# VectorE in source order from the first tile on, and weight halves without GpSimd: attention with a gated MLP on one core

## The chip, the cores and the metric

One core of a Trainium2 chip runs the whole program. The metric is device time in microseconds, the median of the runs of a kernel. All spans, busy times and waits below come from one profiled execution on that core.

## The reference

Attention with a bias that depends on the positions, then a gated MLP on its output. Cut to what matters:

```python
# q, k, v: (4, 8, 576, 64)   w_a, w_b: (512, 1536)   w_out: (1536, 512)
scores = scale * q @ k^T + bias            # bias: a small ReLU net of log1p|i-j| / log1p(i), per head
scores = scores - max(scores)
attn = exp(scores); attn = attn / (sum(attn) + 1e-9)
x = (attn @ v).transpose(0, 2, 1, 3).reshape(4 * 576, 512)
out = ((x @ w_a) * (x @ w_b)) @ w_out      # float32
```

## The kernel before, in words

**Number formats.** To get near float32 accuracy at a 16-bit matmul's pace, `x` and the weights of the MLP's first layer are kept as a scaled fp16 high part and an fp16 low part (the rest), and three products of such parts are added up (L767-771). The second layer does the same with 32-bit halves (`wos`, `gh`, `gl`). The scales are powers of two, found by `pow2_down` and `pow2_up` (L77-95): a maximum per partition, a small matmul that turns it, four tiny VectorE instructions, and a second small matmul with a table of ones (`one`, L877) that spreads the result.

**Attention.** The 144 tiles of 128 query rows run in the generator `attn_steps` (L661-736), two half steps per tile. Of tile n: `qk` makes the scores in PSUM (L502, L511, L525); `soft1` (L532) adds the bias, scales and takes the minimum in one VectorE instruction (L539) and the exponential with its sum on ScalarE (L544); `soft2` (L585) adds 1e-9 on GpSimd (L589), takes the reciprocal on VectorE (L590) and multiplies the tile on GpSimd (L595, for the first 48 tiles; later tiles are split into fp16 parts by L574 and L577); `turn` (L601) transposes the tile on TensorE (L607) and ScalarE copies it out; `pv` and `pv_first` multiply by v (L635, L556). The bias tiles come by DMA, a few tiles ahead.

**Weights.** The first layer's 24 chunks come as float64 and are turned into float32 on the chip. For each chunk `w_unit` (L263) lets ScalarE rescale the high words (L266) and VectorE shift and join bits (L268, L269, L272). `wab_size` (L284) takes the chunk's sum of absolute values on ScalarE (L289), and `wab_parts` (L302) makes the two fp16 parts: GpSimd scales the chunk in place (L306), ScalarE rounds it to fp16 (L309), GpSimd subtracts (L310). `wab_steps` (L320) runs these as a software pipeline of 31 steps. `wo_steps` then brings 12 chunks of the second layer, whose low part GpSimd makes too (L314).

**What sets the order.** Work of `attn_steps`, the weight steps and the MLP blocks (`moe_main`) is woven by `merge` in fixed proportions. TensorE issues in the order in which the program is written from the start (L856). For VectorE, ScalarE and GpSimd a scheduler orders the instructions when the program is built; VectorE too goes over to the written order towards the end of the second MLP block (L970), 46 tiles in. Two rules of `attn_steps` go with that: up to the tile `SOON = 46` the softmax's second half runs one tile late (L734-735), its transposes stand behind the next tile's `qk` (L711-713, L725-726), and the low parts of q, k and v are issued where they are made; from `SOON` on, `soft2(n)` stands ahead of `soft1(n + 1)` (L714-722), the transposes ahead of `qk` (L707-708), and the low parts are put off (`lows`). The first MLP block starts after tile 19, when 13 weight steps have been issued; the other 18 steps of the chunks are woven with its first 20 half steps and 27 half steps of attention (L936-938). Matmuls of `keep` (L885) fill TensorE up to there.

Of the kernel before, what the change touches and what calls it, by code (L numbers as in the profile page):

```python
# [28 lines left out]
FC = DFF // 128  # L29
# [21 lines left out]
SOON = 3 * N0 - 2  # L51
# [3 lines left out]
def attention_moe(ctx, tc, q0d, q1d, kd, vd, idn, wp, wa, wb, wo, lsw, lg, rl, out):  # L55
# [155 lines left out]
    def v_scale(b):  # L211
        mx = wtp[1].tile([128, NP], F32, tag="vmx", name="vmx", bufs=2)
        vfs = [load_v(b, hp) for hp in range(2)] if b else []
        yield
        for hp in range(NP):
            if b:
                junk = vf = vfs[hp]
            else:
                vf = st["vs", hp].rearrange("p x j d -> p (x j d)")
                junk = att.tile([128, 640], F32, tag="rv", name="junk", bufs=2)  # L220
            with late():
                nc.scalar.activation(junk, vf, AF.Abs, accum_out=mx[:, hp:hp + 1])
# [12 lines left out]
        vsc.append(v_scales(pow2_up(dg, 1, "v"), b))  # L235
        yield
# [26 lines left out]
    def w_unit(wt, raw, u=None):  # L263
        lo, hi = raw[:, :, 0], raw[:, :, 1]
        t = wt.tile([128, 512], I32, tag="wt", name="wt", bufs=4)
        nc.scalar.mul(t.bitcast(F32), hi.bitcast(F32), REBIAS)  # L266
        u, s = (t, hi) if u is None else (u, t)
        nc.vector.tensor_scalar(out=u, in0=t, scalar1=3, scalar2=None, op0=ALU.logical_shift_left)  # L268
        nc.vector.scalar_tensor_tensor(  # L269
            out=u, in0=lo, scalar=29, in1=u, op0=ALU.logical_shift_right, op1=ALU.bitwise_or  # L270
        )
        last.append(nc.vector.scalar_tensor_tensor(  # L272
            out=t, in0=s, scalar=-0x80000000, in1=u, op0=ALU.bitwise_and, op1=ALU.bitwise_or
        ))
        return t.bitcast(F32)
# [17 lines left out]
    def wab_scale(p, m):  # L293
# [4 lines left out]
            scalar1=vsc[0][1], scalar2=1.0 / PS, op0=ALU.mult, op1=ALU.mult,  # L298
# [3 lines left out]
    def wab_parts(p, c, wf, rm):  # L302
# [17 lines left out]
    def wab_steps(wt):  # L320
# [14 lines left out]
        fetch_to(3)  # L335
        yield
        for s in range(4 * np_ + 7):
            p, c = divmod(s - 7, 4)
            if 0 <= p < np_:
                if c == 0:  # L340
                    rms[p] = wab_scale(p, pow2_up(dgs.pop(p), 4, "w"))
                with late():
                    wab_parts(p, c, wfs.pop(s - 7), rms[p])
# [8 lines left out]
            if s < 4 * np_:  # L352
                wfs[s] = wab_conv(s, *raws.pop(s))
                fetch_to(s + 1 + min(6, 3 + s // 2))
            yield

    def wo_steps(wt):
        raws = [w_load(wt, wo, f) for f in range(2)]
        yield
        for f in range(FC):  # L360
            with late():
                wf = w_unit(wt, raws[f], wt.tile([128, 512], I32, tag="wt", name="wu", bufs=4))
                wo_split(f, wf)
# [42 lines left out]
    def prep_k(u):  # L406
# [44 lines left out]
    def prep_v(u):  # L451
# [209 lines left out]
    def attn_steps():  # L661
        vgen = [None]
        for n in range(NT + 4):
# [8 lines left out]
            if n <= SOON:  # L672
# [3 lines left out]
            for ahead, un in ((a, TILES[n + a][0]) for a in (6, 4, 3, 1, 0, -1) if 0 <= n + a < NT and FIRST[TILES[n + a][0]] == n + a):  # L676
# [7 lines left out]
                elif ahead == 3:  # L684
                    lows[0] = n >= SOON
# [21 lines left out]
            if SOON <= n < 3 * N0 + 2:  # L707
# [17 lines left out]
            if 2 <= n < SOON:  # L725
                turn(n - 2, tpp)
# [7 lines left out]
            if 1 <= n < SOON:  # L734
                run(soft2(n - 1))
# [135 lines left out]
    with tc.tile_pool(name="bg", bufs=1, side="right") as bg, tc.tile_pool(name="eq", bufs=1, space=PSUM) as eq, \  # L871
# [6 lines left out]
        nc.vector.memset(tab["one"], 1.0)  # L878
# [40 lines left out]
        with tc.tile_pool(name="bh", bufs=1, side="right") as bh:  # L919
# [5 lines left out]
            merge((units, NU0 // 2), (v_scale(0), 7), (wts, 2))  # L925
        keep(8)
# [36 lines left out]
    with tc.tile_pool(name="bg2", bufs=1, reuse_waits="tile") as bg:  # L963
# [6 lines left out]
        ctx.enter_context(tc.manual_schedule(engines={mybir.EngineType.DVE}))  # L970
# [66 lines left out]
```

## Time and profile before

| what | value |
|---|---|
| time, median of 3 runs (lowest, highest) | 752.47 us (751.37, 757.57) |
| the profiled execution's own time | 754.13 us |
| its span, first to last instruction | 752.3 us |
| TensorE matmul busy (share of the span) | 699.4 us (93%) |
| VectorE busy | 497.0 us (66%) |
| ScalarE busy | 449.1 us (60%) |
| GpSimd busy | 333.1 us (44%) |
| mean granted TensorE clock | 0.984 |

PE is TensorE's matmul stream and PEld its weight loads; DVE is VectorE, ACT ScalarE, POOL GpSimd. The granted clock is a share of full speed, 1.00 being 2.4 GHz and 0.50 being 1.2 GHz. A name such as L539 is a line of the kernel before. The shares are means over stages that differ, so the tables by stretch are the ones to read. A wait is put down to what came last: "PE qk L502 <- DVE mn L539" is TensorE standing still before its matmuls of line 502 until the VectorE instruction of line 539 is done.

### The profile page before, as it was taken

Reading aid. Unit: us, or ns where it says so; the run is one execution under the profiler, and the core shown is the slowest. Engines: PE = TensorE matmul, PEld = TensorE weight load, DVE = VectorE, ACT = ScalarE, POOL = GpSimd, SP = SyncE. Lnnn points to the kernel's source line nnn. Section 1 sums busy time; section 2 is a strip of 40 time slices with the busy share of each in tenths; the row PEclk is TensorE's granted clock in tenths of the full one; section 3 lists DMA queues with packets and bytes.
Section 4 is the critical chain, followed back from the end, with each engine's and each line's share of the span. In section 5 each row is a group of like instructions: output and inputs, shape, how many; then the busy total and the mean of one; then the engine's idle time right before and its main releaser. Section 6 shows DMA issues by size and latency. Waiting matters only on the chain.

```text
span 752.3 us, 15601 instructions
## 1 busy us (share of the span) xinstructions
PE 699.4 (93%) x5451; PEld 533.1 (71%) x5451; DVE 497.0 (66%) x1204; ACT 449.1 (60%) x1005; POOL 333.1 (44%) x477
## 2 busy tenths in 40 slices
PE   7787898899899999998899989999999999999997
PEld 2255465577787556676787768878888887888886
DVE  7768688858984576766798888888987781111100
ACT  6868887877876678754555556656655562321310
POOL 3437668865863123332354445634553562311200
PEclk9979999999999999999999999999999999999999
DMA  8998776477754887799999999999999974000001
GB/s 247 322 370 279 241 224 212 147 256 251 248 149 119 219 200 195 187 201 204 246 251 253 225 274 244 248 228 276 246 236 271 222 142 130 1 1 29 2 15 42
DMA packets 178163, 147.69 MB, mean 196 GB/s; under 512 B 125092, under 2 KB 138148, under 8 KB 178084
## 3 DMA queue, kind: packets, MB, share of 16 engines
q1 hardware_dynamic: 170928, 130.92, 69.4%
q10 hardware_dynamic: 5876, 10.93, 5.3%
q0 software_dynamic: 1280, 4.84, 1.8%
q8 instruction: 43, 0.70, 0.4%
q14 instruction: 36, 0.29, 0.1%
HBM read 101.15 MB, written 17.18 MB: 157 GB/s over the span
## 4 chain that ended last, share of the span: by engine, by line
PE 57%; DVE 11%; issue 9%; ACT 9%; POOL 7%; DMA 6%; SPq 0%; ACTq 0%; POOLq 0%; DVEq 0%
PE ab L768 25%; PE o L812 14%; PE pv L635 5%; PE qk L511 4%; DMA pt<-ph 3%; PE psta L155 3%; POOL ph L574 2%; DMA bias<-bias_d 2%; DVE p L539 2%; ACT p L544 2%; PE pr L888 2%; DVE wt L272 2%; PE tp L607 2%; DVE w16t L269 1%; POOL gl L788 1%
## 5 line engine op out<-in xcount | busy, mean ns | idle before, releaser
L768 PEld LDWEIGHTS <-w16t 128*128 128x128 f16 x2592 | 247.1, 98 | 47.1 <-issue 15.8
L768 PE MATMUL ab<-x,w16t 128*128 128x256 f16 x2304 | 270.4, 273 | 3.6 <-DVE x L650 3.3
L544 ACT ACTIVATE p<-p,mn 128x576 f32<-128x576 f32 x144 | 111.6, 775 | 72.9 <-DVE mn L539 63.1
L539 DVE CUSTOM_DVE_ANT_0 p<-qk,bias 128x576 f32<-128x576 f32 x144 | 107.3, 746 | 27.7 <-PE qk L511 11.5
L577 DVE SCALAR_TENSOR_TENSOR ph<-p,sm,ph 128x64 f16<-128x64 f32 x192 | 109.0, 608 | 20.6 <-POOL ph L574 20.0
L574 POOL TENSOR_SCALAR ph<-p,sm 128x576 f16<-128x576 f32 x96 | 71.5, 745 | 115.0 <-DVE sm L590 102.5
L812 PE MATMUL o<-wos,gh 128*128 128x512 f32 x384 | 120.3, 394 | 0.0
L788 POOL TENSOR_TENSOR gl<-g,gh 128x256 fp32r<-128x256 f32 x96 | 73.2, 762 | 89.9 <-ACT gh L787 89.9
L589 POOL TENSOR_SCALAR sm<-sm 128x1 f32<-128x1 f32 x144 | 59.0, 410 | 104.1 <-ACT p L544 99.8
L752 DVE SCALAR_TENSOR_TENSOR g<-ab,wv,asb 128x256 f32<-128x256 f32 x84 | 40.3, 480 | 81.9 <-ACT asb L776 80.7
L787 ACT CAST gh<-g 128x256 fp32r<-128x256 f32 x96 | 38.8, 404 | 75.8 <-DVE g L752 75.7
L812 PEld LDWEIGHTS o<-wos,gh 128*128 128x128 f32 x384 | 69.5, 188 | 16.0 <-issue 3.7
L511 PE MATMUL qk<-ks,qs 128*128 128x288 f32 x384 | 73.6, 313 | 6.0 <-DVE mn L539 4.2
L812 PE MATMUL o<-wos,gl 128*128 128x512 f32 x192 | 75.0, 391 | 0.0
L511 PEld LDWEIGHTS qk<-ks,qs 128*128 128x128 f32 x384 | 56.4, 190 | 16.1 <-DVE mn L539 5.8
L776 ACT ACTIVATE asb<-ab,wv 128x256 f32<-128x256 f32 x84 | 39.4, 469 | 29.0 <-PE ab L768 26.9
L595 POOL TENSOR_SCALAR p<-p,sm 128x576 f32<-128x576 f32 x48 | 43.9, 914 | 26.8 <-DVE sm L590 21.9
L635 PE MATMUL pv<-pt,vs 128*64 128x320 f16 (+1 forms) x560 | 43.5, 310 | 8.6 <-DMA pt<-ph 8.6
L635 PEld LDWEIGHTS <-vs 128*64 128x64 f16 x560 | 32.3, 115 | 21.3 <-issue 9.8
L607 PE MATMUL tp<-idn,p 128*128 128x128 f32 x240 | 38.3, 294 | 5.6 <-ACT ptf L612 4.1
L416 DVE TENSOR_TENSOR ks<-rk,ks 64x576 fp32r<-64x576 f32 x48 | 39.6, 824 | 3.7 <-ACT ks L419 2.2
L818 ACT COPY osb<-o 128x512 f32<-128x512 f32 x18 | 10.5, 583 | 52.2 <-PE o L812 36.4
(102 smaller groups left out, 964.2 us busy)
## 6 DMA issues: line engine op xcount, KB each, us to landing
bias<-bias_d SPq DMA_DIRECT2D x128, 288.0 KB, 3.9
rv<-vd SPq DMA_DIRECT2D x32, 320.0 KB, 4.5
rk<-kd SPq DMA_DIRECT2D x24, 288.0 KB, 3.3
wraw<-wa SPq DMA_DIRECT2D x12, 512.0 KB, 7.4
wraw<-wb SPq DMA_DIRECT2D x12, 512.0 KB, 5.7
wraw<-wo SPq DMA_DIRECT2D x12, 512.0 KB, 4.5
bias_d<-bo ACTq DMA_DIRECT2D x20, 295.5 KB, 3.7
bias_d<-bo POOLq DMA_DIRECT2D x16, 295.5 KB, 6.5
```

The costliest lines, as they stand in the source:

```text
L511: nc.tensor.matmul(ps[:, hf, :HB], a, b[:, hf * HB:hf * HB + HB], start=(x == 0), stop=(x == len(prods) - 1))
L539: ttr = nc.vector.tensor_tensor_reduce(out=p.rearrange("p (a n) -> p a n", a=2), in0=ps[:, :, :HB], in1=bt.rearrange("p (a n) -> p a n", a=2),
L544: exps.append(nc.scalar.activation(p, p, AF.Exp, bias=mn, scale=-1.0, accum_out=sm))
L574: nc.gpsimd.tensor_scalar(out=ph[:, :S], in0=p, scalar1=rc, scalar2=1.0, op0=ALU.mult, op1=ALU.mult)
L577: ins = nc.vector.scalar_tensor_tensor(out=ph[:, o:o + c1 - c0], in0=p[:, c0:c1], scalar=rc, in1=ph[:, c0:c1], op0=ALU.mult, op1=ALU.subtract,
L589: nc.gpsimd.tensor_scalar(out=sm, in0=sm, scalar1=1e-9, scalar2=1.0 / (PS if u >= NF else 1.0), op0=ALU.add, op1=ALU.mult)
L595: nc.gpsimd.tensor_scalar(out=p, in0=p, scalar1=rc, scalar2=1.0, op0=ALU.mult, op1=ALU.mult)
L607: nc.tensor.transpose(tp[:, x, :], p[:, c0:c0 + 128], tab["idn"])
L635: nc.tensor.matmul(ps[64 * j:64 * j + 64, o:o + N], v[:, j, :], p[:, j * N:j * N + N], start=(x == 0), stop=(x == len(prods) - 1),)
L768: nc.tensor.matmul(ab[:, j], w16[nm, f][:, pw, kk, :], xs[px][:, kk, :], start=(x % (3 * KC) == 0), stop=(x % (3 * KC) == 3 * KC - 1),)
L788: nc.gpsimd.tensor_tensor(out=gl, in0=g, in1=gh.bitcast(F32), op=ALU.subtract)
L812: nc.tensor.matmul(o, g[:, sl], wos[f][:, p], start=(f == 0 and x == 0), stop=(f == FC - 1 and x == 2))
```

## The change

Four things, in the words of the diff's names.

1. VectorE issues in written order from the first attention tile on, and the rules that held from tile 46 on hold from tile 0: `turn(n - 2)` ahead of `qk(n + 1)`, then `soft2(n)`'s start, `soft1(n + 1)`, the low parts put off.
2. The first ScalarE instruction of a weight chunk (`w_first`) is issued one step ahead of the chunk's VectorE instructions and writes straight into the tile that these then work on in place; the sign bits come from the raw chunk.
3. `wab_parts` uses no GpSimd: ScalarE multiplies by the scale while it rounds to fp16, and one step later VectorE makes the low part in one multiply-and-subtract. The factor 2^14 goes into the table of ones for that.
4. The weight pipeline gets one more step, and inside a step the chunk's conversion stands first.

```diff
@@ v_scales, tab["one"], wab_scale @@
-        nc.vector.tensor_scalar(out=inv, in0=m, scalar1=1.0 / PS, scalar2=None, op0=ALU.mult)
+        nc.vector.tensor_copy(inv, m)
...
-        nc.vector.memset(tab["one"], 1.0)
+        nc.vector.memset(tab["one"], 1.0 / PS)
...
@@ v_scale @@
         nc.vector.reduce_max(out=m1, in_=mx, axis=AX.X)
+        if b:
+            yield
         dg = pow2_down(m1, 1, "v")
         yield
-        if b:
-            yield
...
@@ weights @@
-    def w_unit(wt, raw, u=None):
-        lo, hi = raw[:, :, 0], raw[:, :, 1]
-        t = wt.tile([128, 512], I32, tag="wt", name="wt", bufs=4)
-        nc.scalar.mul(t.bitcast(F32), hi.bitcast(F32), REBIAS)
-        u, s = (t, hi) if u is None else (u, t)
-        nc.vector.tensor_scalar(out=u, in0=t, scalar1=3, scalar2=None, op0=ALU.logical_shift_left)
+    def w_first(raw, u):
+        nc.scalar.mul(u.bitcast(F32), raw[:, :, 1].bitcast(F32), REBIAS)
+        return u
+
+    def w_unit(raw, u, t):
+        lo, s = raw[:, :, 0], raw[:, :, 1]
+        nc.vector.tensor_scalar(out=u, in0=u, scalar1=3, scalar2=None, op0=ALU.logical_shift_left)
...
@@ wab_parts @@
-        nc.gpsimd.tensor_scalar(
-            out=wv, in0=wv, scalar1=rm[:, c:c + 1], scalar2=PS, op0=ALU.mult, op1=ALU.mult
+        nc.scalar.mul(hi, wv, rm[:, c:c + 1])
+        return lambda: nc.vector.scalar_tensor_tensor(
+            out=lo, in0=wv, scalar=rm[:, c:c + 1], in1=hi, op0=ALU.mult, op1=ALU.subtract
         )
-        nc.scalar.copy(hi, wv)
-        nc.gpsimd.tensor_tensor(out=lo, in0=wv, in1=hi, op=ALU.subtract)
...
@@ wab_steps @@
+        firsts = {0: wab_first(0, raws[0][1])}
         yield
-        for s in range(4 * np_ + 7):
+        low = None
+        for s in range(4 * np_ + 8):
             p, c = divmod(s - 7, 4)
+            if low:
+                low()
+                low = None
+            if s < 4 * np_:
+                pool, raw = raws.pop(s)
+                wfs[s] = wab_conv(pool, raw, firsts.pop(s))
+                pool = raw = None
+                fetch_to(s + 1 + min(6, 3 + s // 2))
+                if s + 1 < 4 * np_:
+                    firsts[s + 1] = wab_first(s + 1, raws[s + 1][1])
...
@@ attn_steps @@
-            if n <= SOON:
+            if n == 0:
                 soft1(n)
...
-            if SOON <= n < 3 * N0 + 2:
+            if 2 <= n < 3 * N0 + 2:
                 turn(n - 2, tpp)
...
-            if SOON <= n <= NT:
-                if n == SOON:
-                    run(soft2(n - 1))
+            if n <= NT:
                 s2 = soft2(n) if n < NT else iter(())
...
-            if 2 <= n < SOON:
-                turn(n - 2, tpp)
...
-            if 1 <= n < SOON:
-                run(soft2(n - 1))
...
@@ main program @@
             merge((units, NU0 // 2), (v_scale(0), 7), (wts, 2))
+        ctx.enter_context(tc.manual_schedule(engines={mybir.EngineType.DVE}))
         keep(8)
...
-        ctx.enter_context(tc.manual_schedule(engines={mybir.EngineType.DVE}))
         merge((main, 2 * FC - 22 + GS + 1), (asteps, n2 - n2 * 5 // 8))
```

VectorE where the first MLP block and the weight chunks run together, before (L268, L269 and L272 are the conversion of a chunk, L539 a tile's first softmax instruction, L590 its reciprocal):

```order
164 L268 TENSOR_SCALAR w16t<-wt 128x512
165 L539 ISA p,mn<-qk,bias 128x576
166 L539 ISA mn 128x1
167 L269 SCALAR_TENSOR_TENSOR w16t<-wraw,w16t 128x512
168 L268 TENSOR_SCALAR w16t<-wt 128x512
169 L272 SCALAR_TENSOR_TENSOR wt<-wt,w16t 128x512
170 L269 SCALAR_TENSOR_TENSOR w16t<-wraw,w16t 128x512
171 L590 RECIPROCAL sm<-sm 128x1
```

and the same place after (L311 is the new low part, L552 and L603 are the old L539 and L590, L80 to L86 the four small instructions of `pow2_down`):

```order
163 L311 SCALAR_TENSOR_TENSOR w16t<-wt,rm,w16t 128x512
164 L268 TENSOR_SCALAR w16t<-w16t 128x512
165 L269 SCALAR_TENSOR_TENSOR w16t<-wraw,w16t 128x512
166 L272 SCALAR_TENSOR_TENSOR wt<-wraw,w16t 128x512
167 L80 TENSOR_REDUCE p2m<-pr 4x1
168 L81 TENSOR_SCALAR p2m<-p2m 4x1
169 L82 TENSOR_SCALAR p2m<-p2m 4x1
170 L86 TENSOR_SCALAR p2d<-idn,p2m 4x4
171 L603 RECIPROCAL sm<-sm 128x1
172 L552 ISA p,mn<-qk,bias 128x576
173 L552 ISA mn 128x1
```

The instructions of two chunks and a tile are no longer mixed; a chunk stands in one piece with a low part in front, and a tile's reciprocal stands directly ahead of the next tile's first instruction.

TensorE near the end of the first stage, before (L502 makes the next tile's scores, L607 are the transposes of an earlier tile, L888 the filling matmuls):

```order
137 L888 LDWEIGHTS w16t
138 L888 MATMUL pr<-w16t 128x512
139 L502 MATMUL qk<-rkf,rqf 128x288 x2
140 L607 MATMUL tp<-idn,p 128x128 x5
141 L888 LDWEIGHTS w16t
```

and after (L620 is the old L607, L515 the old L502, L893 the old L888):

```order
139 L893 LDWEIGHTS w16t
140 L893 MATMUL pr<-w16t 128x512
141 L620 MATMUL tp<-idn,p 128x128 x5
142 L515 MATMUL qk<-rkf,rqf 128x288 x2
143 L893 LDWEIGHTS w16t
```

The transposes have moved ahead of the matmuls that wait for VectorE.

GpSimd in the stretch of the weight chunks, before (L306 and L310 make a chunk's parts, L589 and L595 belong to the softmax):

```order
59 L306 TENSOR_SCALAR wt<-wt,rm 128x512
60 L589 TENSOR_SCALAR sm<-sm 128x1
61 L595 TENSOR_SCALAR p<-p,sm 128x576
62 L310 TENSOR_TENSOR w16t<-wt,w16t 128x512 x2
63 L589 TENSOR_SCALAR sm<-sm 128x1
64 L595 TENSOR_SCALAR p<-p,sm 128x576
65 L306 TENSOR_SCALAR wt<-wt,rm 128x512 x3
```

and after (L602 and L608 are the old L589 and L595):

```order
47 L602 TENSOR_SCALAR sm<-sm 128x1
48 L608 TENSOR_SCALAR p<-p,sm 128x576
49 L602 TENSOR_SCALAR sm<-sm 128x1
50 L608 TENSOR_SCALAR p<-p,sm 128x576
51 L602 TENSOR_SCALAR sm<-sm 128x1
```

Only the softmax's two instructions per tile are left there.

## Rows read from the trace of the kernel before

**Rows 1.** Busy us by stretch: PE, PEld, DVE, ACT, POOL, clock, DMA share, GB/s.

```profile
36.00:62.00 26.00, 22.03 (x143) 13.93 (x139) 18.62 (x50) 18.12 (x43) 9.51 (x17) 0.80 0.92 338
62.00:99.30 37.30, 32.47 (x255) 19.49 (x255) 26.62 (x78) 32.37 (x76) 28.42 (x39) 1.00 0.81 264
99.30:138.60 39.30, 34.90 (x273) 24.02 (x270) 35.28 (x82) 31.10 (x71) 28.09 (x33) 1.00 0.66 208
138.60:166.50 27.90, 24.59 (x188) 18.45 (x188) 16.66 (x45) 22.98 (x49) 21.31 (x28) 0.94 0.61 203
166.50:235.00 68.50, 64.42 (x519) 52.69 (x520) 55.62 (x116) 52.12 (x111) 44.60 (x52) 0.98 0.69 214
235.00:330.00 95.00, 89.83 (x708) 59.95 (x706) 61.22 (x151) 69.71 (x151) 24.75 (x40) 1.00 0.78 184
```

**Rows 2.** TensorE's waits, 36 to 235 us: total us, times, longest us.

```profile
PE qk L502 <- DVE mn L539: 5.1, 3, 2.5
PE qk L511 <- DVE mn L539: 4.2, 4, 2.6
...
PE qk L525 <- DVE mn L539: 1.3, 2, 0.7
```

**Rows 3.** TensorE's waits, 235 to 330 us, the largest.

```profile
PE psta L155 <- DVE g L752: 1.7, 2, 1.2
```

**Rows 4.** VectorE by group, 99.3 to 138.6 us: busy us, mean ns.

```profile
L269 DVE SCALAR_TENSOR_TENSOR w16t<-wraw,w16t 128x512 int32<-128x512 int32 x11 | 9.9, 898 | 0.0
L272 DVE SCALAR_TENSOR_TENSOR wt<-wt,w16t 128x512 int32<-128x512 int32 x11 | 9.6, 872 | 0.0
L268 DVE TENSOR_SCALAR w16t<-wt 128x512 int32<-128x512 int32 x11 | 6.4, 579 | 1.8 <-ACT wt L266 1.8
...
L590 DVE RECIPROCAL sm<-sm 128x1 f32<-128x1 f32 x8 | 1.2, 153 | 1.7 <-POOL sm L589 1.7
```

**Rows 5.** Instructions in order of time, 129 to 134 us: start us, us.

```profile
129.37 2.79 POOL L310 TENSOR_TENSOR w16t<-wt,w16t 128x512 f16<-128x512 f32 x2
...
131.06 1.65 DVE L269 SCALAR_TENSOR_TENSOR w16t<-wraw,w16t 128x512 int32<-128x512 int32 x1
...
133.30 0.42 DVE L268 TENSOR_SCALAR w16t<-wt 128x512 int32<-128x512 int32 x1
...
133.64 0.68 DVE L272 SCALAR_TENSOR_TENSOR wt<-wt,w16t 128x512 int32<-128x512 int32 x1
```

**Rows 6.** GpSimd by group, 99.3 to 138.6 us.

```profile
L310 POOL TENSOR_TENSOR w16t<-wt,w16t 128x512 f16<-128x512 f32 x9 | 11.7, 1314 | 0.3
L595 POOL TENSOR_SCALAR p<-p,sm 128x576 f32<-128x576 f32 x8 | 7.9, 991 | 5.1 <-DVE sm L590 3.7 <-PE tp L607 1.4
L306 POOL TENSOR_SCALAR wt<-wt,rm 128x512 f32<-128x512 f32 x8 | 5.9, 744 | 3.9 <-DVE rm L295 3.9
L589 POOL TENSOR_SCALAR sm<-sm 128x1 f32<-128x1 f32 x8 | 3.1, 382 | 1.2 <-ACT p L544 0.6
```

**Rows 7.** VectorE by group and shape, whole run: the nearest form to the new instruction.

```profile
L577 DVE SCALAR_TENSOR_TENSOR ph<-p,sm,ph 128x512 f16<-128x512 f32 x96 | 71.4, 743 | 0.0
```

**Rows 8.** The first tile's softmax in order of time, 36 to 39 us.

```profile
36.47 0.76 DVE L539 CUSTOM_DVE_ANT_0 p<-qk,bias 128x576 f32<-128x576 f32 x1 [3.15 <-PE qk L525]
...
37.27 0.78 ACT L544 ACTIVATE p<-p,mn 128x576 f32<-128x576 f32 x1 [2.81 <-DVE mn L539]
...
38.24 0.19 POOL L589 TENSOR_SCALAR sm<-sm 128x1 f32<-128x1 f32 x1 [2.94 <-ACT p L544]
38.46 0.16 DVE L590 RECIPROCAL sm<-sm 128x1 f32<-128x1 f32 x1 [0.54 <-POOL sm L589]
```

**Rows 9.** VectorE's waits, 166.5 to 235 us, the largest.

```profile
DVE sm L590 <- POOL sm L589: 6.5, 6, 2.1
```

**Rows 10.** GpSimd by group, 166.5 to 235 us, the largest.

```profile
L314 POOL TENSOR_TENSOR wos<-wt,wos 128x512 fp32r<-128x512 f32 x12 | 18.2, 1523 | 5.0 <-ACT wos L313 5.0
```

More of the change, by code (lines that the diff above doesn't have):

```diff
@@ L50 @@
 VS = N0 - 4, 2 * N0 - 4, 3 * N0 - 10
-SOON = 3 * N0 - 2
 @with_exitstack
@@ L278, in attention_moe, with wab_first, wab_conv @@
     w16t = cst.tile([128, FC, 2, 2, KC, 128], F16, name="w16t")
-    def wab_conv(n, wt, raw):
+    def wab_first(n, raw):
         with late():
-            return w_unit(wt, raw, w16t[:, n // 2, n % 2].rearrange("p x k n -> p (x k n)").bitcast(I32))
+            return w_first(raw, w16t[:, n // 2, n % 2].rearrange("p x k n -> p (x k n)").bitcast(I32))
+    def wab_conv(wt, raw, u):
+        with late():
+            return w_unit(raw, u, wt.tile([128, 512], I32, tag="wt", name="wt", bufs=4))
     def wab_size(f, j, wf, m):
@@ L297, in wab_scale @@
             out=winv[:, 2 * p:2 * p + 2, :], in0=m.rearrange("p (f j) -> p f j", j=2),
-            scalar1=vsc[0][1], scalar2=1.0 / PS, op0=ALU.mult, op1=ALU.mult,
+            scalar1=vsc[0][1], scalar2=None, op0=ALU.mult,
         )
@@ L342, in wab_steps @@
                 with late():
-                    wab_parts(p, c, wfs.pop(s - 7), rms[p])
+                    low = wab_parts(p, c, wfs.pop(s - 7), rms[p])
             p, c = divmod(s - 5, 4)
@@ L351, in wab_steps, with first @@
                 wab_size(2 * p + c // 2, c % 2, wfs[s - 1], ms[p])
-            if s < 4 * np_:
-                wfs[s] = wab_conv(s, *raws.pop(s))
-                fetch_to(s + 1 + min(6, 3 + s // 2))
             yield
     def wo_steps(wt):
+        def first(f):
+            with late():
+                return w_first(raws[f], wt.tile([128, 512], I32, tag="wt", name="wu", bufs=4))
         raws = [w_load(wt, wo, f) for f in range(2)]
+        t = first(0)
         yield
@@ L361, in wo_steps @@
             with late():
-                wf = w_unit(wt, raws[f], wt.tile([128, 512], I32, tag="wt", name="wu", bufs=4))
+                wf = w_unit(raws[f], t, t)
                 wo_split(f, wf)
-            raws[f] = None
+            raws[f] = t = wf = None
             if f + 2 < FC:
                 raws.append(w_load(wt, wo, f + 2))
+            if f + 1 < FC:
+                t = first(f + 1)
             yield
     st = {}
-    lows = [False, []]
+    lows = []
     def lows_now(k=9):
-        for _ in range(min(k, len(lows[1]))):
-            lows[1].pop(0)()
+        for _ in range(min(k, len(lows))):
+            lows.pop(0)()
     def load_unit(u):
@@ L419, in prep_k @@
             nc.scalar.copy(ks[sl, j], rk[sl])
-            lows[1].append(partial(low, j))
-        if not lows[0]:
-            lows_now()
+            lows.append(partial(low, j))
         st["ks", u] = ks
@@ L433, in prep_q @@
         nc.scalar.copy(d[:, 0], s)
-        lows[1].append(
+        lows.append(
             lambda: nc.vector.tensor_tensor(out=d[:, 1], in0=s, in1=d[:, 0].bitcast(F32), op=ALU.subtract)
         )
-        if not lows[0]:
-            lows_now()
         st["qs", u] = dst
@@ L460, in prep_v @@
         nc.scalar.mul(hi, rv, vsc[UNITS[u][0]][0])
-        lows[1].append(lambda: nc.vector.scalar_tensor_tensor(
+        lows.append(lambda: nc.vector.scalar_tensor_tensor(
             out=lo, in0=rv, scalar=vsc[UNITS[u][0]][0], in1=hi, op0=ALU.mult, op1=ALU.subtract
         ))
-        if not lows[0]:
-            lows_now()
         st["vs", u] = vs
```

2 lines of the change are left out of this document (removed).

## The prediction, made before the changed kernel was run

> **What bounds the kernel now.** I read the table of busy time by stretch first, then each engine's waits in the stretches that the change touches, then the groups of VectorE and GpSimd there, and last the instructions in order of time around a few long ones. The stretches are cut close to where tiles 10, 20, 28, 34 and 48 begin.
>
> The table [rows 1] shows two kinds of stretch. From 235 us on, TensorE is busy 89.8 of 95 us, and the waits left there are small [rows 3]: nothing ahead of it is late. Between 36 and 235 us it is busy 178.4 of 199 us, so it stands still for 20.6, and at 0.80, 0.94 and 0.98 of the clock in three stretches it also runs below full speed. That is all that a better order can win, because the number of matmuls is the same after the change.
>
> Who makes it wait differs. From 99.3 to 138.6 us VectorE is busy 35.3 of 39.3 us [rows 1]: eight tiles, and eleven weight chunks to convert [rows 4]. VectorE is the bound of this stretch. From 138.6 to 166.5 us VectorE has little to do (16.7 of 27.9), while GpSimd is busy 21.3 and ScalarE 23.0. From 166.5 to 235 us TensorE is at 64.4 of 68.5 again. The waits agree: matmuls that wait for a tile's first softmax instruction cost TensorE 5.1, 4.2 and 1.3 us [rows 2], 10.6 in all.
>
> VectorE's own time is stretched by GpSimd. One L269 takes 1.65 us where it meets the subtraction L310, a like instruction 0.68 us where it does not [rows 5]. In the busy stretch the means of L269, L272 and L268 are 0.898, 0.872 and 0.579 us [rows 4]. Against 0.68, 0.68 and 0.42 [rows 5] this is 0.22, 0.19 and 0.16, times eleven 6.3 us.
>
> **The change part by part.** *GpSimd's share of the chunk parts goes to ScalarE and VectorE.* Removed are 24 each of L306 and L310. ScalarE's rounding stays and gets a factor, at no cost that I can see: it is one instruction on the same tile as before. Added are 24 multiply-and-subtract instructions on VectorE. The nearest form, with the same shapes and types, takes 0.743 us [rows 7], so 17.8 us in all. Counted in the order against the tiles, 5 of them fall in 62 to 99.3 us, 11 in 99.3 to 138.6 and 8 in 138.6 to 166.5.
>
> In the bound stretch this is 11 x 0.743 = 8.2 us. What comes back is the stretching by L306 and L310. They are 17.6 of GpSimd's 28.6 us there [rows 6], so I give them 62% of 6.3, or 3.9 us. VectorE's load becomes 35.3 + 8.2 - 3.9 = 39.6 us in a stretch of 39.3. So the stretch cannot get shorter, unless all the stretching goes (35.3 + 8.2 - 6.3 = 37.2, a gain of 2.1). It gets longer by as much of its present 4.0 us of VectorE's idle time as stays (43.6, a loss of 4.3). Some of these waits have lost their reason: the 1.8 us for ScalarE's first instruction, which is now a step ahead, and the 1.7 us for GpSimd [rows 4], which now has the softmax only. So I take +0.5.
>
> The lock between the two engines is also the place where the Trainium skill speaks against the change. Its page "SBUF — State Buffer", section "Who interferes with whom", says that a VectorE instruction with two inputs in SBUF and a GpSimd instruction that reads SBUF shut each other out for a whole instruction, and the new instruction is of that kind. The row of 1.65 us agrees with it [rows 5]. By the rule, if each of the 24 met a softmax multiplication L595 (0.991 us, [rows 6]) half way, 24 x 0.5 = 12 us would be added to the 17.8; the sum goes by the mean stretching in the rows instead.
>
> From 62 to 99.3 us, 5 x 0.743 = 3.7 us of new work stand against 10.7 us in which VectorE is idle [rows 1]. I take that as hidden and give the order -0.5 there (bounds -4.8, TensorE's idle time, and +3.7, all of the new work in the open). From 138.6 to 166.5 us, 8 x 0.743 = 5.9 us stand against 11.2 us of idle VectorE, and the queue of GpSimd, on which a tile's normalization had to wait behind L306 and L310, is gone. TensorE stands still for 3.3 us there, and 0.94 of the clock over 27.9 us is another 1.7. I take half of the two, -2.5 (bounds -5.0 and, with the new work uncovered, +5.9).
>
> *VectorE in written order; transposes ahead of the scores; the softmax's end ahead of the next tile.* The same rules hold before the change from tile 46 on, and there TensorE's waits for L539 are gone [rows 3]. The transposes now fill the time in which TensorE waited for L539. The price is that VectorE stands before the reciprocal of a tile until ScalarE's exponential and GpSimd's L589 are through, and all that follows is queued behind: the next tile's first instruction, hence TensorE's next scores. On the first tile this chain takes from 36.47 to 38.62 us, 2.15 us [rows 8], and a tile takes 2.6 us there (ten tiles start in the 26 us of that stretch). With a chunk's conversion between (0.42 + 0.68 + 0.68 = 1.8 us) most of the wait is covered. So the first stretch neither gains nor loses much by it: -0.5, with -4.0 (TensorE's idle time) and -5.2 (its clock) together as the lower bound and +2 as the upper, an estimate from ten tiles that each lose 0.2.
>
> From 166.5 to 235 us the chunks of the second layer are converted, GpSimd still makes their low parts, and only the order changes. TensorE's idle time is 4.1 us and its clock costs 0.02 x 68.5 = 1.4. I take -1.5 (bounds -5.5, and +8.7, worked out below).
>
> *Chunks one step ahead, one more weight step, the scale in the table of ones.* No instruction is added on the path. The parts of a chunk are ready four steps before the MLP asks for them, so one step later costs nothing; without that cover it would be one step, some 3 us, once. After 235 us nothing changes: 0 (bounds -1 and +1, since the loads on SP's queue keep nearly their order).
>
> Sum: -0.5 - 0.5 + 0.5 - 2.5 - 1.5 = -4.5 us. The profiled execution took 754.13 us (span 752.3 and 1.8 around it), so 749.6 for it. It lies 1.7 above the median of 752.47, and for a median I forecast **748.0 us**.
>
> **The rivals.** *A: the order works everywhere (738.8).* TensorE's waits for L539 go (10.6 us, [rows 2]) and with them the lower clock after 138.6 us (1.7 + 1.4): -13.7. For it: from 235 us on, the same order shows no such wait. Against it: there VectorE is busy 61 of 95 us, and in the bound stretch it is full.
>
> *B: VectorE becomes the bound for good (760.7).* Place: 99.3 to 138.6 us. The port that L306 and L310 leave is taken up by new meetings of the low parts with L595, nothing comes back, and 8.2 us stand in the open. It decides if the mean of L269 and L272 there stays near 0.88 us. For it: VectorE has 4 us left there, and a low part and a conversion in one piece, 2.5 us, stand ahead of each softmax. Against it: 62% of GpSimd's work there is gone.
>
> *C: VectorE stuck behind GpSimd's subtractions (some 758).* Place: 166.5 to 235 us. L314 takes 1.523 us, twelve times [rows 10]; six reciprocals wait behind GpSimd there for 6.5 us already [rows 9], 1.1 each. In the written order what follows cannot pass. If all 14 tiles wait so, 8 x 1.1 = 8.7 us more; with the 3 us that the other stretches give, +5.7. It decides if that wait doubles.
>
> *D: no change worth the name (752.5).* Chunks keep their places between the tiles almost to the tile in both orders, so the written order moves little, and VectorE's new load in the bound stretch eats what the next one gives.
>
> The Trainium skill would make the move itself dearer or cheaper by little: "GPSIMD Engine Reference", section "Performance versus the Vector engine", calls VectorE about twice as fast for such work, which from L310's 1.314 us [rows 6] would make the low part 0.66 and the 11 of them 7.2 us, not 8.2. No row here shows this instruction on VectorE yet.
>
> **How the numbers follow.** Forecast 0.40, A 0.18, B 0.11, C 0.09, D 0.22. A measurement of this kernel can tell about 1%, or 7.5 us, from no change. Faster by more: A, and a third of the forecast's spread, 0.31. Slower by more: B, and most of C, 0.20. The rest, 0.49, is within. The range from 739 to 760 leaves out the far half of A and of B.
>
> **What would show it.** Right: the mean of L269 and L272 in the chunk stretch falls to about 0.75 us, the new instruction takes about 0.74, VectorE is over 95% busy there; TensorE's waits for L539 shrink below 5 us; the stretch from tile 28 to tile 34 is 2 to 3 us shorter. Wrong: tiles 20 to 28 take more than 42 us (B), the wait for L589 after tile 34 grows beyond 10 us (C), or the time from tile 48 to the end is not what it was.

## The result, and the profile after

| | before | after |
|---|---|---|
| time, median of 4 runs (lowest, highest) | 754.73 us (751.37, 757.57) | 763.28 us (761.84, 765.37) |
| profiled execution, its span | 754.13, 752.3 us | 761.84, 760.0 us |
| VectorE, GpSimd busy | 497.0, 333.1 us | 507.6, 279.0 us |

The ratio is 1.0119, with a 95% interval from 1.0083 to 1.0155. The change makes the kernel slower by about 9 us, and 763 lies outside the range of 739 to 760.

In the code after, L515 and L552 are what L502 and L539 were before; likewise L576/L577 for L563/L564, L602/L603 for L589/L590, L608 for L595, L78 to L93 for L79 to L94, and L893 for the fillers L888. L310 is ScalarE's high part of a chunk and L311 the new low part on VectorE.

The busy time by stretch of the kernel after, cut where the tiles 10, 20, 28, 34 and 48 begin in it (columns as in [rows 1]):

```profile
64.60:110.80 46.20, 35.73 (x230) 20.45 (x227) 27.35 (x80) 30.16 (x68) 10.91 (x20) 0.82 0.60 195
110.80:154.70 43.90, 37.79 (x279) 26.24 (x278) 36.97 (x93) 33.65 (x75) 8.67 (x16) 0.92 0.59 188
154.70:176.80 22.10, 20.56 (x172) 16.09 (x171) 15.42 (x42) 19.30 (x42) 6.48 (x13) 1.00 0.58 176
176.80:248.20 71.40, 65.58 (x541) 52.95 (x539) 62.33 (x125) 54.09 (x115) 43.34 (x53) 1.00 0.70 227
```

Before, tile 10 began at 65.5 us and the same four pieces took 33.8, 39.3, 27.9 and 69.4 us. So tiles 10 to 20 lost 12.4 us, tiles 20 to 28 lost 4.6, tiles 28 to 34 won 5.8, and tiles 34 to 48 lost 2.0. What lies ahead won 0.9 and what lies behind 4.6; together +7.7, the difference of the spans. The forecast, in the same order, was -0.5 ahead of tile 10, then -0.5, +0.5, -2.5, -1.5 and 0. In the first two pieces no engine is full: VectorE is busy 27 of 46 and 37 of 44 us. The time went into waits and into a lower clock, 0.82 and 0.92.

TensorE's and VectorE's waits from 84 to 124 us, kernel after:

```profile
PE pr L893 <- DVE p2m L80: 4.4, 1, 4.4
PE pr L893 <- DVE p2g L93: 2.4, 1, 2.4
...
DVE p L552 <- PE qk L515: 7.4, 3, 3.0
DVE x L577 <- ACT x L576: 5.2, 2, 3.0
DVE w16t L311 <- ACT w16t L310: 1.9, 1, 1.9
```

Most of VectorE's 7.4 us for the scores lie behind TensorE's two standstills, not ahead of them. The kernel before has these two as well, but short (TensorE's waits from 65.5 to 99.3 us):

```profile
PE pr L888 <- DVE p2g L94: 0.8, 1, 0.8
...
PE pr L888 <- DVE p2m L81: 0.4, 1, 0.4
```

They have nothing to do with the softmax. They belong to the exchange of a scale between the partitions (TensorE transposes maxima by L78, VectorE reduces them by L80 to L86, TensorE spreads the result by L91, VectorE copies it by L93). It has one PSUM tile, `pr`, which the fillers use too. The largest wait in order of time, all engines, kernel after:

```profile
97.19 0.65 ACT L263 ACTIVATE w16t<-wraw 128x512 f32<-128x512 f32 x1
...
97.66 0.38 PE L78 MATMUL pr<-idn,vm 128*1 128x128 f32 x2
97.75 0.71 ACT L310 ACTIVATE w16t<-wt,rm 128x512 f16<-128x512 f32 x1
...
98.36 0.61 ACT L293 ACTIVATE w16t<-wt 128x512 f16<-128x512 f32 x1
...
98.97 0.35 ACT L576 ACTIVATE x<-pv,vs 128x128 f16<-128x128 f32 x1
99.35 0.35 DVE L577 SCALAR_TENSOR_TENSOR x<-pv,vs,x 128x128 f16<-128x128 f32 x1 [3.02 <-ACT x L576]
99.62 0.74 DVE L311 SCALAR_TENSOR_TENSOR w16t<-wt,rm,w16t 128x512 f16<-128x512 f32 x1
...
101.46 0.69 DVE L272 SCALAR_TENSOR_TENSOR wt<-wraw,w16t 128x512 int32<-128x512 int32 x1
102.07 0.27 DVE L80 TENSOR_REDUCE p2m<-pr 1x1 f32<-1x128 f32 x1
...
102.39 1.01 PE L893 MATMUL pr<-w16t 128*128 128x512 f16 x2 [4.36 <-DVE p2m L80]
...
103.20 1.27 PE L620 MATMUL tp<-idn,p 128*128 128x128 f32 x5
```

L78 is through at 98.04 us. Its answer L80 takes 0.27 us, and comes at 102.07. Ahead of it in VectorE's written order stands the low part of x, L577, which waits 3.02 us because ScalarE does three instructions for the chunks before L576; behind that come the low part of a chunk and a conversion, 2.7 us with L577. VectorE stands idle while L80 is ready. TensorE, whose order is written too, stands before the filler that needs `pr`, and the transposes and scores behind the filler wait with it. That VectorE takes its instructions strictly first in, first out is what the Trainium skill says too ("TensorE: Matmul & The Clock Gate", the table that opens it); the 4.0 us in which L80 was ready and did not run agree.

The first wait, 2.44 us, is for L93:

```profile
84.41 0.38 PE L91 MATMUL pr<-p2d,one 4*128 4x4 f32 x2
...
84.57 0.74 DVE L311 SCALAR_TENSOR_TENSOR w16t<-wt,rm,w16t 128x512 f16<-128x512 f32 x1
...
87.02 0.15 DVE L93 COPY p2g<-pr 128x4 f32<-128x4 f32 x1
...
87.23 1.01 PE L893 MATMUL pr<-w16t 128*128 128x512 f16 x2 [2.44 <-DVE p2g L93]
```

L91 is through at 84.79, and L93 comes at 87.02, behind a low part and a conversion; no input is late there, the work ahead is only long. After this wait four groups of matmuls run at half the clock: L893, L620, L515 and L569 take 1.01, 1.27, 1.33 and 2.60 us, where a kernel without this wait (below) has 0.59, 0.71, 0.76 and 1.46. That is 2.7 us more, so this wait costs about twice its length. After the second wait, of 4.36 us, the next four groups take 4.6 us instead of 2.7, 2.0 more. The granted clock is 0.50 from 87 to 93 us, and 0.73 from 84 to 104.

### The profile page after: what moved, and what is told of

Same layout as the page of the kernel before. It is cut to its first block, busy times and chain, and to the rows that moved or that the text cites. A ratio compares the mean times of both kernels' runs of the same rounds, so it can differ in the third digit from the quotient of the medians.

```text
span 760.0 us, 15593 instructions
## 1 busy us (share of the span) xinstructions
PE 699.6 (92%) x5451; PEld 532.2 (70%) x5451; DVE 507.6 (67%) x1228; ACT 450.9 (59%) x1005; POOL 279.0 (37%) x429
## 4 chain that ended last, share of the span: by engine, by line
PE 54%; DVE 11%; issue 11%; ACT 11%; POOL 7%; DMA 5%; SPq 0%; ACTq 0%; POOLq 0%; DVEq 0%
PE ab L773 23%; PE o L817 14%; PE pv L648 5%; POOL ph L587 4%; PE qk L524 3%; PE psta L154 3%; ACT p L557 2%; POOL sm L602 2%; DVE p L552 2%; POOL gl L793 1%; PE tp L620 1%; DVE ph L590 1%; ACT w16t L293 1%; ACT w16t L263 1%; DVE ks L435 1%
## 5 line engine op out<-in xcount | busy, mean ns | idle before, releaser
L552 DVE CUSTOM_DVE_ANT_0 p<-qk,bias 128x576 f32<-128x576 f32 x144 | 107.1, 744 | 26.5 <-PE qk L524 11.3
L590 DVE SCALAR_TENSOR_TENSOR ph<-p,sm,ph 128x64 f16<-128x64 f32 x192 | 109.3, 609 | 21.8 <-POOL ph L587 20.8
L602 POOL TENSOR_SCALAR sm<-sm 128x1 f32<-128x1 f32 x144 | 59.6, 414 | 126.9 <-ACT p L557 125.5
L524 PEld LDWEIGHTS qk<-ks,qs 128*128 128x128 f32 x384 | 56.2, 189 | 12.4 <-issue 5.4
L608 POOL TENSOR_SCALAR p<-p,sm 128x576 f32<-128x576 f32 x48 | 36.5, 761 | 73.9 <-DVE sm L603 72.4
L648 PE MATMUL pv<-pt,vs 128*64 128x320 f16 (+1 forms) x560 | 41.5, 301 | 6.8 <-DMA pt<-ph 6.8
L620 PE MATMUL tp<-idn,p 128*128 128x128 f32 x240 | 37.1, 288 | 10.4 <-ACT ptf L625 5.0
L620 PEld LDWEIGHTS tp<-idn,p 128*128 128x128 f32 x240 | 28.7, 148 | 18.6 <-issue 11.8
L817 PEld LDWEIGHTS o<-wos,gl 128*128 128x128 f32 x192 | 36.0, 188 | 7.8
```

The source lines that it names most:

```text
L524: nc.tensor.matmul(ps[:, hf, :HB], a, b[:, hf * HB:hf * HB + HB], start=(x == 0), stop=(x == len(prods) - 1))
L552: ttr = nc.vector.tensor_tensor_reduce(out=p.rearrange("p (a n) -> p a n", a=2), in0=ps[:, :, :HB], in1=bt.rearrange("p (a n) -> p a n", a=2),
L590: ins = nc.vector.scalar_tensor_tensor(out=ph[:, o:o + c1 - c0], in0=p[:, c0:c1], scalar=rc, in1=ph[:, c0:c1], op0=ALU.mult, op1=ALU.subtract,
L602: nc.gpsimd.tensor_scalar(out=sm, in0=sm, scalar1=1e-9, scalar2=1.0 / (PS if u >= NF else 1.0), op0=ALU.add, op1=ALU.mult)
L620: nc.tensor.transpose(tp[:, x, :], p[:, c0:c0 + 128], tab["idn"])
L648: nc.tensor.matmul(ps[64 * j:64 * j + 64, o:o + N], v[:, j, :], p[:, j * N:j * N + N], start=(x == 0), stop=(x == len(prods) - 1),)
```

## The experiments

The table has the kernel after (763.28 us, beside 754.73 before) and fourteen experiments, with ratios to runs of the kernel before on the same chip (median 754.5 for the first four experiments, 754.1 for the next four, 753.7 for four more, 755.3 for the last two). The kernel after, e1, e5 and e9 have four runs each, so their intervals are the widest; the others have eight or ten. The last columns say how much later than in the kernel before a tile begins, in the trace.

| kernel | median us | ratio (95%) | tile 20 | tile 34 | tile 143 |
|---|---|---|---|---|---|
| after | 763.28 | 1.0119 (1.0083 to 1.0155) | +11.5 | +10.3 | +7.8 |
| e1_order_only | 766.38 | 1.0173 (1.0107 to 1.0239) | +10.6 | +12.0 | +12.0 |
| e2_parts_only | 749.56 | 0.9945 (0.9921 to 0.9968) | +1.5 | -3.4 | -5.5 |
| e3_no_fill | 758.76 | 1.0064 (1.0036 to 1.0092) | +5.6 | +4.3 | +5.4 |
| e4_pow2_first | 762.02 | 1.0107 (1.0074 to 1.0140) | +9.6 | +8.7 | +9.0 |
| e5_x_late | 765.74 | 1.0166 (1.0112 to 1.0221) | +7.0 | +9.6 | +11.8 |
| e6_both | 757.67 | 1.0062 (1.0034 to 1.0089) | +3.6 | +2.5 | +3.3 |
| e9_rules_only | 745.24 | 0.9895 (0.9848 to 0.9942) | -1.8 | -6.7 | -8.8 |
| e8_from_19 | 754.81 | 1.0015 (0.9986 to 1.0043) | -1.1 | +0.2 | 0.0 |
| e10_low_mid | 751.35 | 0.9959 (0.9931 to 0.9986) | -1.5 | -5.5 | -3.3 |
| e11_until_19 | 757.64 | 1.0046 (1.0010 to 1.0083) | +8.4 | +3.5 | +4.9 |
| e12_all_mends | 758.76 | 1.0064 (1.0032 to 1.0097) | +3.1 | -0.2 | +4.7 |
| e13_no_order | 751.82 | 0.9969 (0.9943 to 0.9996) | -1.0 | -4.2 | +3.7 |
| e14_until_19_mended | 752.65 | 0.9967 (0.9936 to 0.9997) | +2.1 | +0.6 | -1.2 |
| e15_rules_mended | 747.99 | 0.9907 (0.9873 to 0.9942) | 0.0 | -2.8 | -3.1 |

**The two parts of the change, one at a time.** The kernel after with GpSimd making the chunk parts again:

```diff
-        nc.scalar.mul(hi, wv, rm[:, c:c + 1])
-        return lambda: nc.vector.scalar_tensor_tensor(
-            out=lo, in0=wv, scalar=rm[:, c:c + 1], in1=hi, op0=ALU.mult, op1=ALU.subtract
-        )
+        nc.gpsimd.tensor_scalar(
+            out=wv, in0=wv, scalar1=rm[:, c:c + 1], scalar2=1.0, op0=ALU.mult, op1=ALU.mult
+        )
+        nc.scalar.copy(hi, wv)
+        nc.gpsimd.tensor_tensor(out=lo, in0=wv, in1=hi, op=ALU.subtract)
```

> The changed kernel with the chunk parts made on GpSimd again (scale, round on ScalarE, subtract). Theory 1 (the written order makes VectorE read the small maxima in the one PSUM bank `pr` late, TensorE stands before the filling matmuls that use the same bank, and its clock falls): the loss stays, 760 to 766 us, and tiles 16 to 22 again take some 40 us instead of 25. Theory 2 (the 24 new low parts overload VectorE, rival B): the loss goes, 752 to 756 us.

And the kernel before with only that edit in the other direction, VectorE's order left to the scheduler up to tile 46:

> The kernel before with only the chunk parts moved to ScalarE and VectorE, all in the scheduler's order. Theory 1: no loss, 748 to 756 us, no wait of TensorE for the bank `pr` above 1 us. Theory 2: the loss of the changed kernel is here too, 760 us or more, in tiles 20 to 28.

The first is no better than the kernel after (3.1 us more, intervals that overlap), the second is faster than before. So the chunk parts are a gain, and VectorE becoming the bound (rival B) is out. The gain is where the prediction put it in tiles 28 to 34, which take 24.9 us in e2_parts_only (27.9 before). Tiles 20 to 28 take 37.4 (39.3 before), a gain of 1.9 where the forecast was a loss of 0.5. Its rows from 100.8 us, where tile 20 begins in it:

```profile
100.80:138.20 37.40, 34.46 (x270) 23.77 (x269) 35.97 (x91) 31.84 (x71) 13.61 (x16) 1.00 0.68 223
138.20:163.10 24.90, 23.90 (x195) 18.10 (x192) 20.18 (x53) 22.78 (x49) 6.19 (x12) 1.00 0.67 222
```

**Which place in the order.** Without the fillers between the tiles (`keep(2)` left out; they are matmuls whose result nothing reads):

```diff
-        merge((asteps, 4), (wts, 1), ((keep(2) for _ in range(4)), 4))
+        merge((asteps, 4), (wts, 1))
...
-        merge((asteps, n0), (wts, 3), ((keep(2) for _ in range(n0)), n0))
+        merge((asteps, n0), (wts, 3))
```

> The changed kernel without the filling matmuls that are woven into the tiles (those ahead of the first tile stay); they compute nothing that is used. Theory 1: the waits before them (2.4 and 4.4 us) go and the transposes behind them run on, 750 to 756 us, unless the clock falls for want of work, which the table by stretch would show. Theory 2: no change, 761 to 765 us.

And with the two halves of the chunks' exchange called ahead of the low part and the conversion in a weight step:

```diff
             p, c = divmod(s - 7, 4)
+            if 0 <= p < np_ and c == 0:
+                rms[p] = wab_scale(p, pow2_up(dgs.pop(p), 4, "w"))
+            if 0 <= s - 5 < 4 * np_ and (s - 5) % 4 == 0:
+                dgs[(s - 5) // 4] = pow2_down(ms.pop((s - 5) // 4), 4, "w")
             if low:
```

> The changed kernel with the small instructions on the chunk scales (both pow2 helpers) at the head of a weight step, ahead of the low part and the conversion. Theory 1: VectorE reads the bank early, the waits of TensorE for it shrink from 6.8 us to under 3, 752 to 758 us. Theory 3 (VectorE stands before the low part of x, line 577, until ScalarE has its high part, 5.2 us in the bad stretch, and all else is late from that): little change, 759 to 765 us, and the 4.4 us wait, which is for the scale of v, stays.

Without fillers the same standstill lies before the exchange itself (TensorE waits 4.2 us at L91): the fillers are not the cause. But the wait of 2.4 us is gone, and the time of 758.76 us, 4.5 better than after, lies between what the two theories said. With the chunks' exchange first, its wait falls from 2.4 to 0.3 us, but the one for the scale of v stays (TensorE's waits from 84 to 124 us, e4_pow2_first; its lines are one less than after):

```profile
PE pr L892 <- DVE p2m L80: 4.4, 1, 4.4
...
PE pr L892 <- DVE p2g L93: 0.3, 1, 0.3
```

That answer stands behind x. So the low part of x was put behind the next tile's first softmax instruction, alone and with the edit above:

```diff
-        nc.vector.scalar_tensor_tensor(
+        xlate.append(lambda: nc.vector.scalar_tensor_tensor(
             out=xl, in0=ps[:, :128], scalar=vsc[0][0], in1=xh, op0=ALU.mult, op1=ALU.subtract
-        )
+        ))
...
                 lows_now(2)
+                while xlate:
+                    xlate.pop(0)()
```

> The low part of x is issued behind the next tile's first softmax instruction instead of at once. Theory 1 (the answers to the scale exchanges stand behind the rounded-weight and chunk work in VectorE's written order, and TensorE stands before the next user of the one bank): VectorE's 3.0 us wait for ScalarE's x goes, the answer for v's scale comes some 3 us earlier, and TensorE's 4.4 us wait falls to 1 to 2 us, but 2.5 us of chunk work stays ahead of it: 757 to 761, tile 22 some 10 to 13 us behind the kernel before instead of 16. Theory 3 (the low part of x at the head of VectorE's queue is the cost by itself): both of its waits, 5.2 us, go and TensorE's clock recovers with them: 752 to 756, tile 22 less than 7 us behind.

> The low part of x late and the scale exchange's two halves at the head of the weight step, together. Theory 1: what stands ahead of the answers is gone, TensorE waits under 2 us in total for them between 84 and 110 us, and the time comes to 750 to 756. Rival (the cost is the written order as such: VectorE in one order cannot follow a TensorE that is early or late by some us, whichever instruction stands at the head): the wait moves to another instruction, 758 to 763.

Alone it is a miss: the 4.4 us fall to 0.4, tile 22 is 11.4 us late instead of 16.2, yet the time is no better than after; tile 28 is 15.3 us late, so the next tiles do not keep what was won. Together the two edits win 5.6 us, to 757.67, between the two ranges expected. TensorE's two waits are down to 0.4 and 0.3 us, as theory 1 had it, and yet the kernel stays 3.6 us slower than before: these standstills are a part of the loss, not all of it.

**The order itself.** The kernel after with the one line that demands VectorE's written order moved back to its old place (tile 46), or (e8_from_19) to the start of the first MLP block, ahead of tile 20:

```diff
-        ctx.enter_context(tc.manual_schedule(engines={mybir.EngineType.DVE}))
         keep(8)
...
+        ctx.enter_context(tc.manual_schedule(engines={mybir.EngineType.DVE}))
         merge((main, 2 * FC - 22 + GS + 1), (asteps, n2 - n2 * 5 // 8))
```

> The changed kernel, all its code as it is, but VectorE's written order is demanded only from the place where it was demanded before; the scheduler orders VectorE up to there. If the written order of VectorE is the cost: 746 to 752, as the kernel with the chunk parts alone (749.6) or better. If the attention step's changed calls (the turn ahead of the scores, the first half of the softmax a step earlier) are the cost, whoever orders VectorE: 758 to 765.

> As the changed kernel, but VectorE's written order begins at the first MLP's start, and the scheduler orders VectorE in tiles 0 to 19. If the loss lies in the tiles ahead of that place alone: 748 to 753. If the exchanges of the tiles behind it cost as much: 756 to 760, with the loss now between tiles 20 and 28.

This decides it. All else of the change, with the scheduler's order on VectorE up to tile 46, gives 745.24 us: 9 us faster than before. The written order adds 18 us to that (11 to 23 by the ends of the two intervals). The 754.81 of e8_from_19 lies between its two ranges: both stretches cost. The same place as above, in e9_rules_only:

```profile
90.09 0.66 ACT L263 ACTIVATE w16t<-wraw 128x512 f32<-128x512 f32 x1
...
90.56 0.38 PE L78 MATMUL pr<-idn,vm 128*1 128x128 f32 x2
...
90.64 0.72 ACT L310 ACTIVATE w16t<-wt,rm 128x512 f16<-128x512 f32 x1
...
91.17 0.27 DVE L80 TENSOR_REDUCE p2m<-pr 1x1 f32<-1x128 f32 x1
91.26 0.62 ACT L293 ACTIVATE w16t<-wt 128x512 f16<-128x512 f32 x1
91.39 1.01 DVE L311 SCALAR_TENSOR_TENSOR w16t<-wt,rm,w16t 128x512 f16<-128x512 f32 x1
91.49 0.59 PE L893 MATMUL pr<-w16t 128*128 128x512 f16 x2 [0.56 <-DVE p2m L80]
...
91.87 0.36 ACT L576 ACTIVATE x<-pv,vs 128x128 f16<-128x128 f32 x1
...
92.39 0.33 DVE L577 SCALAR_TENSOR_TENSOR x<-pv,vs,x 128x128 f16<-128x128 f32 x1
```

ScalarE's order at this place is the same as in the kernel after. Only VectorE's differs: L80 follows L78 at 0.23 us instead of 4.03, and L577 comes when its input is there. TensorE waits 0.56 us instead of 4.36, and is busy 19.3 of 20 us from 84 to 104, at full clock.

One rival is not quite out. The scheduler orders ScalarE and GpSimd too, and when VectorE's order is fixed it places them a little differently. Counted in the traces, TensorE's order is the same in after and e9_rules_only, but some 60 of ScalarE's 1005 instructions and 23 of GpSimd's 429 stand elsewhere, most of them behind 120 us. Between e11_until_19 (below) and e9_rules_only it is 12 and 1, so what e11_until_19 costs is VectorE's order almost alone. Of the rest, how much is ScalarE's and GpSimd's order was not tested.

**Two stretches.** Written order from tile 20 on costs 9.6 us (754.81 against 745.24). Its waits are of the same kind: in tiles 20 to 28 of e8_from_19 VectorE stands 4.9 us before the low part of a chunk for ScalarE's high part, with conversion, softmax and gate behind. So the low part was put ahead of the third instruction of the next conversion instead of the first; and for the other stretch the written order was demanded in tiles 0 to 19 alone.

```diff
             out=u, in0=lo, scalar=29, in1=u, op0=ALU.logical_shift_right, op1=ALU.bitwise_or
         )
+        if mid:
+            mid()
+        if callable(t):
+            t = t()
```

> As e8_from_19 (written order from tile 20 on; 754.8), but the low part of a chunk stands between the second and the third instruction of the next chunk's conversion instead of ahead of the first, so that 1.1 us of ready work lies ahead of it. Theory 1 (the cost is that ready work stands behind an instruction whose input is late): VectorE's 4.9 us wait for ScalarE's high part between tiles 20 and 28 falls to about 2, the softmax and the gate behind it come earlier, and the time to 750 to 753. Rival (that wait is the same delay seen in another place, since ScalarE and TensorE are in orders of their own): it moves to the gate or to x, 754 to 757.

> The complement of e8_from_19: written order of VectorE in tiles 0 to 19 only, the scheduler's order from the first MLP on to the old place. If the costs of the two stretches add (763.3 - 754.8 = 8.5 us for tiles 0 to 19, over the 745.2 of the kernel without either): 751 to 756. If the scheduler takes back what the first stretch lost, since VectorE has room behind it: 746 to 750. If the first stretch alone brings on all of the loss: 758 to 763.

VectorE's waits in tiles 20 to 28, e8_from_19:

```profile
DVE w16t L311 <- ACT w16t L310: 4.9, 3, 1.9
DVE x L663 <- ACT x L661: 3.4, 2, 3.1
```

The same of e10_low_mid:

```profile
DVE w16t L315 <- ACT w16t L314: 2.7, 3, 1.4
DVE x L668 <- ACT x L666: 0.2, 1, 0.2
```

That wins 3.5 us, to 751.35, as theory 1 expected. The order in tiles 0 to 19 alone costs 12.4 us (757.64 against 745.24), above the 751 to 756 expected if the costs add. The two stretches add up to 22.0, where the order in both costs 18.0, a difference that the intervals do not resolve.

**All three edits together, with the written order, in part of the program, and without it.**

> The changed kernel with written order everywhere, and the three places mended: x late, the exchange's halves at the head of the weight step, the low part inside the next conversion. Theory 1: 757.7 for the first two, less the 2 to 4 us that the third gives: 752 to 756. Rival (what is written cannot follow the others' delays): 757 to 760.

> The written order in tiles 0 to 19 only, as in e11_until_19 (757.6), with the three mends. If the late inputs at VectorE's head are all that this order costs in that stretch: back to 746 to 750. If they are half of it: 751 to 754. If the mends only move the delay: 755 or more.

> The three mends in the kernel whose VectorE is ordered by the scheduler up to the old place (745.2 without them). If the mends cost nothing by themselves: 743 to 748, and what the written order still costs with them (758.8) is the order's. If they cost something, since x and the low parts are ready later: 750 or more, and the 758.8 is partly theirs.

With the order in tiles 0 to 19 the edits win 5.0 us (757.64 to 752.65, in the range expected if they are half of the cost). In the trace they win more at that place: tile 20 begins 10.2 us later with the written order than without it when nothing is mended (+8.4 against -1.8), and 2.1 us later when it is (+2.1 against 0.0). So in the traces four fifths of the loss up to tile 20 came from what stood at the three places; by the medians, 12.4 us of loss without the edits and 4.7 with them (752.65 against 747.99), it is three fifths. The edits seem to cost something themselves (747.99 against 745.24, intervals that overlap). With the order everywhere they win 4.5 us and leave 10.8 (758.76 against 747.99): that is a miss, in the range of the rival and not of theory 1. The third edit, worth 3.5 us from tile 20 on, added nothing to the two in e6_both. Tile 34 is 2.7 us earlier, but between tiles 62 and 143 that kernel loses 3.5 us. In that stretch all kernels but e13_no_order have the same written order, and their traces still differ there, from -4.1 us (after) to +3.5; why stays open. So does which instructions make up the 10.8 us left.

**No written order anywhere.**

> The changed kernel with no written order of VectorE anywhere: the scheduler orders it in the last 500 us too, where the kernel before also had the written order. If the written order costs wherever ScalarE's results are late: 738 to 744. If in that stretch VectorE's order is not what TensorE waits for (no wait of TensorE above 1.7 us there before): 744 to 747. If the written order pays there: 748 or more.

Here it pays: without it the kernel is 6.6 us slower than e9_rules_only. In the traces all of that lies behind tile 100. From tile 48 to tile 100 e13_no_order takes 226.0 us and e9_rules_only 228.6. From tile 100 to tile 143 they take 163.9 and 151.6 (the profiled execution of e13_no_order was the slowest of its ten, 754.78 us). TensorE's waits between tiles 100 and 143 in e13_no_order:

```profile
PE qk L524 <- DVE mn L552: 5.1, 6, 1.2
PE ab L773 <- DVE g L757: 3.0, 3, 2.0
```

and in e9_rules_only:

```profile
PE ab L773 <- DVE g L757: 0.2, 1, 0.2
```

## Why the prediction was wrong

**The step that failed** is the pricing of "VectorE in written order", in tiles 10 to 20 above all. The prediction gave it -0.5 us in 62 to 99.3, with +3.7 as the upper bound ("all of the new work in the open"); tiles 10 to 20 lost 12.4. Between 99.3 and 166.5 us it gave the order no price at all, and from tile 20 on the order cost 9.6 (e8_from_19). It named one instruction at which VectorE would stand, the reciprocal behind ScalarE's exponential and GpSimd's L589, and counted as queued behind it the next tile's softmax. It did not go through the other heads of the queue that wait for ScalarE (x, the low part of a chunk), nor the short answers to TensorE that stand behind those. The wait that it did name did not grow: VectorE stood 14.9 us before the reciprocal for GpSimd between 36 and 235 us, and stands 8.6 us there after. A wait does not show as work, so the busy times by which the bound was made could not hold it: e9_rules_only does the same work and takes 35.9 us for tiles 10 to 20, 2.1 more than before, within that bound. The other 10.3 us came with the order.

**"No instruction is added on the path"** was said of the chunks one step ahead and of the scale. True, but L80 and L93 were on TensorE's path all along, and the new order moved work ahead of them.

**The inference from [rows 3]**, that the same order had cleared the waits from tile 46 on and would do so earlier, carried over only in part. TensorE's waits for L552 between 36 and 235 us fell from 10.6 to 7.6 us, not below 5 as the text had it (kernel after):

```profile
PE qk L515 <- DVE mn L552: 2.8, 3, 1.6
PE qk L538 <- DVE mn L552: 2.6, 3, 1.8
...
PE qk L524 <- DVE mn L552: 2.2, 2, 2.0
```

In the later stretch the order does pay, by 6.6 us. But there are no exchanges of scales and no chunks of the first layer in that stretch.

**The chunk parts were right, some better than forecast.** VectorE by group in tiles 20 to 28, kernel after:

```profile
L311 DVE SCALAR_TENSOR_TENSOR w16t<-wt,rm,w16t 128x512 f16<-128x512 f32 x11 | 8.7, 787 | 4.9 <-ACT w16t L310 4.9
L269 DVE SCALAR_TENSOR_TENSOR w16t<-wraw,w16t 128x512 int32<-128x512 int32 x10 | 6.9, 692 | 0.3
L272 DVE SCALAR_TENSOR_TENSOR wt<-wraw,w16t 128x512 int32<-128x512 int32 x10 | 6.9, 692 | 0.3
...
L268 DVE TENSOR_SCALAR w16t<-w16t 128x512 int32<-128x512 int32 x10 | 4.1, 414 | 0.0
```

L269, L272 and L268 are back at 0.69, 0.69 and 0.41 us: all 6.3 us of the stretching of [rows 4] went, not 62% of it, and the new instruction takes 0.79 against 0.743. In e2_parts_only the three take 0.773, 0.711 and 0.409 us over the same tiles, so some 1.3 of the 6.3 us stay there. The gain of 2.5 us in tiles 28 to 34 is 3.0 in e2_parts_only. "VectorE over 95% busy" came true in e2_parts_only (36.0 of 37.4 us), not after (84%).

**The rivals.** B gave nearly the right time (760.7) for a wrong reason, and its first sign (tiles 20 to 28 above 42 us) came true, with 43.9. Its other sign, means that stay near 0.88 us, did not: they are 0.69. C is out: from 177 to 248 us VectorE has no wait for L602 at all. A's 738.8 wanted an order that works everywhere; e9_rules_only comes to 745.24. D (no change) is out: the interval is clear of 1.

**By the rule of the Trainium skill** ("SBUF — State Buffer", "Who interferes with whom") the new instruction would meet GpSimd's multiplications, which the prediction put at 12 us for 24 of them. Over the whole run of the kernel after they took 0.775 us each against the 0.743 of [rows 7], 0.8 us for all 24. The rule agrees with e9_rules_only, where an L311 beside L608 took 1.01 us, but in the kernel after meetings are rare, with GpSimd busy 8.7 of 43.9 us in tiles 20 to 28.

## What to carry to other kernels

Before an engine's order is fixed by hand, list every instruction in it that waits for another engine, and ask at each what stands behind it that a third engine is waiting for. Short answers (a reduce of 0.3 us that frees a PSUM tile) belong ahead of long work and of anything whose input may be late. Fix the order by stretches and measure each: here it lost 18 us in the first 230 us and won 6.6 in the rest, behind tile 100, and the best kernel, 745.24 us, has it only there.

## What the runs showed of the hardware

In the kernel after, a standstill of TensorE of 2.4 us, with two shorter ones of 0.9 and 0.55 us ahead of it, was followed by 6.2 us of matmuls at 1.2 GHz (granted clock 0.50), 2.7 us more than the same matmuls took at 2.4 GHz in e9_rules_only. One of 4.4 us was followed by 4.6 us of them, 2.0 us more. Counted by its own length alone, the first would be priced at about half of what it cost, the second at about two thirds.
